# Moving operands of two FFNs laid out as even and odd tokens, and read as the two halves in turn

## The chip, the core and the metric

The kernel runs on one core of one Trainium2 chip. The metric is device time in microseconds of that core, from one launch. TensorE's records show two levels of its clock, 1.2 and 2.4 GHz; a granted clock of 1.00 in the profile is the upper one.

## What is computed

```
qn = q / (norm(q, axis=1) + 1e-6);  kn = k / (norm(k, axis=1) + 1e-6)     # 6016 x 256
a  = softmax(kn.T @ qn / tau)                                             # 256 x 256
x  = v @ a                                                                # 6016 x 256
h  = x @ w_in1;  x = (h * cos(h)) @ w_out1                                # 256 -> 2048 -> 256
h  = x @ w_in2;  out = (h * sigmoid(h)) @ w_out2                          # 256 -> 2048 -> 256
```

All inputs are float32 (the weights are handed over as 64-bit words and decoded on the chip).

## The kernel before

**Scores.** q and k stream in; 188 plain float32 matmuls (L247, moving operand 256 columns) add up the 256 x 256 score matrix. After the softmax the attention is folded into the first weights: `emit_w` (L342, plain float32, 512 columns) makes `wa` = attention times `w_in1`, so that v itself is the input of the first FFN.

**Tokens.** Everything is held transposed: features on the partitions, tokens along the free dimension. The 6016 tokens are cut into 12 blocks, four of 512 and eight of 496 tokens (`SIZES`). The moving operand of a matmul is a stretch of tokens, the stationary one a 128 x 128 tile of weights.

**Three passes.** Both FFNs compute in `float32r`, a rounded float32, with each operand split in two: `hi` is the rounded value, `lo` the rounded rest. A product is three matmuls (`PASSES`): weight hi by data hi, weight lo by data hi, weight hi by data lo. The splits of v are made on GpSimd (`split_v`; the first block's `hi` on ScalarE), those of everything later with `hi` on ScalarE (L409 in FFN 1, L441 in `part_hi`) and `lo` on VectorE (L410, L444 in `part_lo`).

**FFN 1.** A unit is (block b, m) with m = 0..7, so 96 units. `emit_h` (L381) makes two 128-row slices of h with 12 matmuls; ScalarE and VectorE form h*cos(h) and split it; `emit_o1` (L420), two units later, adds it into the output with 12 more. Each of these matmuls has a block's 512 or 496 columns. There are 4 x 8 x 24 = 768 with 512 columns and 8 x 8 x 24 = 1536 with 496.

**FFN 2.** It multiplies 2 x 2 blocks with seven products instead of eight (`PRODUCTS`), with operands formed by sums and differences (`forms_first`, `forms_second`). A block's two halves of tokens are the columns of the 2 x 2 data blocks, so a matmul (L484, in `product`) has 256 or 248 columns. `emit_x2` forms the inputs and stores them in DRAM while FFN 1 runs, `load_x2` brings them back. A unit is 7 products x 3 passes on the way in and as many on the way out: 42 matmuls, 4 x 8 x 42 = 1344 of 256 columns and 8 x 8 x 42 = 2688 of 248. The last output is finished by `emit_plain` (L523).

**Order.** The schedule is written out by hand: program order is the order in each engine's queue. Units are pipelined with a lag of two (FFN 1) or three (FFN 2), so that TensorE has the next unit's matmuls while ScalarE and VectorE work on the last one. Every matmul is preceded by the load of its own weights (PEld in the profile), which runs while the matmul ahead of it streams.

## Time and profile before

| | |
|---|---|
| median of 3 runs | 1084.74 us |
| lowest and highest | 1083.97 and 1087.33 us |
| profiled execution, first to last instruction | 1086.1 us |
| TensorE busy, share of the span | 98% |
| VectorE, ScalarE, GpSimd busy | 84%, 69%, 30% |
| mean granted TensorE clock | 0.993 |

The profiled execution's own time is given as its span alone; it lies between the lowest and the highest run. A busy share counts the time in which at least one instruction of the engine is under way. Matmuls overlap: one takes some 280 to 400 ns from its start to its end, but the next starts after 113 to 230 ns. So what a matmul costs is the time from its start to the start of the next one, which is read from the chain of waits (its pieces hold so many matmuls end to end) or from the length of a stretch divided by the matmuls in it.

### The profile page before, as it was taken

The numbers are of one execution on the slowest core, as the hardware profiler recorded it, in microseconds if no ns is written. First come the engines' busy times: TensorE is split into PE (matmuls) and PEld (weight loads), VectorE is DVE, ScalarE is ACT, GpSimd is POOL, SyncE is SP. The second block draws the span as 40 slices with busy tenths as digits, with TensorE's granted clock in tenths as the row PEclk, the third lists the DMA queues.
The fourth block names the chain that finished last, engine by engine and source line by source line (L and its number), as shares of the span: only waits on it lengthen the run. The fifth ranks groups of instructions, "written<-read, shape, count | busy, mean of one in ns | idle before, by whom it ended". The sixth has DMA issues, their size and how long they took to land.

```text
span 1086.1 us, 17011 instructions
## 1 busy us (share of the span) xinstructions
PE 1060.6 (98%) x6593; PEld 946.7 (87%) x6593; DVE 915.4 (84%) x1177; ACT 747.2 (69%) x1182; POOL 321.3 (30%) x301
## 2 busy tenths in 40 slices
PE   8888999999999999999999899999999999999998
PEld 7746788888888888888888699999999999999998
DVE  6979998878878888887677588898889889888987
ACT  6555666666666666666566578778778787787785
POOL 2257555535743455450100011111111111111110
PEclk9989999999999999999999999999999999999999
DMA  9712212243152332431127651211220220222001
GB/s 350 284 53 81 76 40 88 97 169 121 53 179 82 110 119 89 155 119 43 43 75 276 221 204 68 89 33 60 81 82 15 76 85 17 70 86 67 29 11 39
DMA packets 56544, 109.49 MB, mean 101 GB/s; under 512 B 2832, under 2 KB 37648, under 8 KB 56464
## 3 DMA queue, kind: packets, MB, share of 16 engines
q1 hardware_dynamic: 56320, 108.28, 29.3%
q8 instruction: 52, 0.85, 0.3%
q14 instruction: 28, 0.23, 0.1%
q10 hardware_dynamic: 144, 0.13, 0.0%
HBM read 68.75 MB, written 39.65 MB: 100 GB/s over the span
## 4 chain that ended last, share of the span: by engine, by line
PE 89%; DVE 8%; ACT 1%; DMA 1%; issue 0%; SPq 0%; DVEq 0%; ACTq 0%
PE h L381 23%; PE o L420 22%; PE o L484 21%; PE xz L484 12%; PE ys L484 9%; DVE acc L275 2%; PE pw L342 1%; DVE lo L410 1%; DMA qk<-qk_dram 1%; DVE t L394 1%; DVE t L402 1%; DVE wv_wo L140 1%; DVE wv_wo L144 0%; DVE wv_wo L141 0%; SPq L259 0%
## 5 line engine op out<-in xcount | busy, mean ns | idle before, releaser
L444 DVE TENSOR_TENSOR lo<-t,hi 128x744 fp32r<-128x744 f32 (+3 forms) x190 | 208.1, 1096 | 44.5 <-ACT hi L441 42.9
L484 PE MATMUL o<-hi,wo 128*128 128x248 f32 (+1 forms) x1330 | 238.6, 278 | 0.0
L381 PE MATMUL h<-xhi,wa 128*128 128x496 f32 (+1 forms) x768 | 207.9, 393 | 2.8 <-DVE wa L350 2.8
L436 POOL TENSOR_TENSOR t<-t 128x248 f32<-128x248 f32 (+1 forms) x94 | 68.3, 727 | 476.6 <-DVE t L435 421.4
L420 PE MATMUL o<-hi,wo 128*128 128x496 f32 (+1 forms) x768 | 206.6, 391 | 0.0
L441 ACT ACTIVATE hi<-t 128x744 fp32r<-128x744 f32 (+3 forms) x190 | 178.7, 941 | 40.2 <-PE o L484 39.5
L484 PEld LDWEIGHTS o<-hi,wo 128*128 128x128 f32 x1330 | 201.9, 189 | 0.0
L393 ACT ACTIVATE t<-h 128x992 int32<-128x992 f32 (+1 forms) x96 | 96.8, 1008 | 132.8 <-PE h L381 126.7
L394 DVE SCALAR_TENSOR_TENSOR t<-t,h 128x992 f32<-128x992 int32 (+1 forms) x96 | 114.9, 1197 | 84.3 <-ACT t L393 83.8
L484 PE MATMUL o<-lo,wo 128*128 128x248 f32 (+1 forms) x665 | 184.8, 278 | 0.0
L381 PEld LDWEIGHTS h<-xhi,wa 128*128 128x128 f32 x768 | 145.1, 189 | 34.9 <-ACT wv_wo L136 3.6
L420 PEld LDWEIGHTS o<-hi,wo 128*128 128x128 f32 x768 | 144.6, 189 | 30.7
L401 ACT ACTIVATE t<-t,half_pi 128x992 f32<-128x992 f32 (+1 forms) x96 | 109.1, 1137 | 65.3 <-DVE t L394 65.3
L484 PE MATMUL xz<-x2hi,wi 128*128 128x248 f32 (+1 forms) x768 | 146.6, 278 | 0.0
L410 DVE TENSOR_TENSOR lo<-t,hi 128x992 fp32r<-128x992 f32 (+1 forms) x96 | 135.3, 1409 | 1.2 <-ACT hi L409 1.2
L484 PEld LDWEIGHTS o<-lo,wo 128*128 128x128 f32 x665 | 125.5, 189 | 0.0
L420 PE MATMUL o<-lo,wo 128*128 128x496 f32 (+1 forms) x384 | 119.4, 392 | 5.6 <-DVE lo L410 5.6
L402 DVE TENSOR_TENSOR t<-h,t 128x992 f32<-128x992 f32 (+1 forms) x96 | 115.1, 1199 | 6.9 <-ACT t L401 1.2
L381 PE MATMUL h<-xlo,wa 128*128 128x496 f32 (+1 forms) x384 | 119.1, 392 | 0.0
L484 PEld LDWEIGHTS xz<-x2hi,wi 128*128 128x128 f32 x768 | 116.8, 189 | 0.2
L484 PE MATMUL ys<-x2hi,wi 128*128 128x248 f32 (+1 forms) x576 | 113.6, 279 | 3.1 <-ACT u L758 2.7
L484 PE MATMUL xz<-x2lo,wi 128*128 128x248 f32 (+1 forms) x384 | 106.8, 278 | 0.0
(129 smaller groups left out, 1660.4 us busy)
## 6 DMA issues: line engine op xcount, KB each, us to landing
qk<-qk_dram SPq DMA_DIRECT2D x22, 512.0 KB, 8.5
raw_wo<-w_out_dram SPq DMA_DIRECT2D x16, 512.0 KB, 5.2
xshi<-yhi SPq DMA_DIRECT2D x8, 868.0 KB, 6.2
xslo<-ylo SPq DMA_DIRECT2D x8, 868.0 KB, 6.6
x2hi<-xshi SPq DMA_DIRECT2D x8, 868.0 KB, 5.3
x2lo<-xslo SPq DMA_DIRECT2D x8, 868.0 KB, 7.6
wo_dram<-stage_wo SPq DMA_DIRECT2D x7, 896.0 KB, 4.7
wo<-wo_dram SPq DMA_DIRECT2D x7, 896.0 KB, 7.4
```

The costliest lines, as they stand in the source:

```text
L275: nc.vector.tensor_tensor(out=acc[:, :n], in0=acc[:, :n], in1=sq[:, :n], op=ALU.add)
L381: nc.tensor.matmul(hp[:, s, :n], lhsT, rhs, start=(i == 0), stop=(i == len(todo) - 1))
L393: nc.scalar.activation(k, hp[:, :, :n], AF.Copy, scale=1.0 / TWO_PI, bias=0.25)
L394: nc.vector.scalar_tensor_tensor(out=t[:, :, :n], in0=k, scalar=-TWO_PI, in1=hp[:, :, :n], op0=ALU.mult, op1=ALU.add)
L401: nc.scalar.activation(t[:, :, :n], t[:, :, :n], AF.Sin, bias=half_pi)
L402: nc.vector.tensor_tensor(out=t[:, :, :n], in0=hp[:, :, :n], in1=t[:, :, :n], op=ALU.mult)
L410: nc.vector.tensor_tensor(out=lo[:, :, :n], in0=t[:, :, :n], in1=hi[:, :, :n].bitcast(F32), op=ALU.subtract)
L420: nc.tensor.matmul(o[:, e, :n], wo1_at(i, f)[:, e * P : (e + 1) * P], parts[k][:, s, :n], start=(f == 0 and (i, k) == PASSES[0]), stop=(f ...
L436: eng.tensor_tensor(out=t[:, 7, :c], in0=t[:, 3, :c], in1=t[:, 6, :c], op=ALU.subtract)
L441: nc.scalar.activation(hi[:, sl, :c], t[:, 1:][:, sl, :c], AF.Copy)
L444: nc.vector.tensor_tensor(out=lo[:, sl, :c], in0=t[:, 1:][:, sl, :c], in1=hi[:, sl, :c].bitcast(F32), op=ALU.subtract)
L484: nc.tensor.matmul(out, w[:, p, ka - 1], x[r][:, kb - 1, : out.shape[-1]], start=(start and i == 0), stop=(stop and i == 2), skip_group_ch ...
```

## The change

`hi` and `lo` of every FFN matmul get another order in SBUF. Before, column j of the operand is token j of the stretch. After, the first half of the stretch holds the even tokens 0, 2, 4, ... and the second half the odd ones. The matmul's access pattern then reads element 0 of the first half, element 0 of the second, element 1 of the first, and so on, so that TensorE gets the tokens in their old order; results in PSUM, everything behind them and the output are where they were.

Three views do it. `turns` is the source in a split, read with a step of two elements (8 bytes): first the even ones, then the odd ones. `halves` is the same tile's destination, each half written contiguously. `columns` is what the matmul reads: the inner dimension has 2 elements that lie half a stretch apart (1024 or 992 bytes in FFN 1, 512 or 496 bytes in FFN 2), the outer one steps by 4 bytes.

```
+    def columns(t):
+        return t.rearrange("p (h b) -> p b h", h=2)
+    def halves(t):
+        return t.rearrange("p s (h b) -> p s h b", h=2)
+    def turns(t):
+        return t.rearrange("p s (b h) -> p s h b", h=2)
...
-            nc.scalar.activation(hi[:, :, :n], raw[:, :, :n], AF.Copy)
+            nc.scalar.activation(halves(hi[:, :, :n]), turns(raw[:, :, :n]), AF.Copy)
...
-                out=hi[:, :, :n], in0=raw[:, :, :n], scalar1=1.0, scalar2=1.0, op0=ALU.mult, op1=ALU.mult
+                out=halves(hi[:, :, :n]), in0=turns(raw[:, :, :n]), scalar1=1.0, scalar2=1.0, op0=ALU.mult, op1=ALU.mult
...
-            todo = [(wa_at(i, a, 2 * m + s), x[k][:, a, :n]) for i, k in PASSES for a in range(CH)]
+            todo = [(wa_at(i, a, 2 * m + s), columns(x[k][:, a, :n])) for i, k in PASSES for a in range(CH)]
...
-        nc.vector.tensor_tensor(out=lo[:, :, :n], in0=t[:, :, :n], in1=hi[:, :, :n].bitcast(F32), op=ALU.subtract)
+        nc.vector.tensor_tensor(
+            out=halves(lo[:, :, :n]), in0=turns(t[:, :, :n]), in1=halves(hi[:, :, :n]).bitcast(F32), op=ALU.subtract
+        )
...
-                parts[k][:, s, :n],
+                columns(parts[k][:, s, :n]),
...
-        nc.scalar.activation(hi[:, sl, :c], t[:, 1:][:, sl, :c], AF.Copy)
+        nc.scalar.activation(halves(hi[:, sl, :c]), turns(t[:, 1:][:, sl, :c]), AF.Copy)
...
-                x[r][:, kb - 1, : out.shape[-1]],
+                columns(x[r][:, kb - 1, : out.shape[-1]]),
```

The other edits (the `lo` of `split_v` and of `part_lo`, the last unit's split, `emit_plain`) are of the same kind. The numbers of instructions, their engines, their order, their sizes and the transfers stay as they were.

## Rows read from the trace of the kernel before

**Rows 1.** The page: busy time of each engine, and the granted clock in 40 slices.
```profile
PE 1060.6 (98%) x6593; PEld 946.7 (87%) x6593; DVE 915.4 (84%) x1177; ACT 747.2 (69%) x1182; POOL 321.3 (30%) x301
PEclk9989999999999999999999999999999999999999
```

**Rows 2.** The page: the chain that ended last, shares by engine and by line.
```profile
PE 89%; DVE 8%; ACT 1%; DMA 1%; issue 0%; SPq 0%; DVEq 0%; ACTq 0%
PE h L381 23%; PE o L420 22%; PE o L484 21%; PE xz L484 12%; PE ys L484 9%; DVE acc L275 2%; PE pw L342 1%; DVE lo L410 1%; DMA qk<-qk_dram 1%; DVE t L394 1%; DVE t L402 1%; DVE wv_wo L140 1%; DVE wv_wo L144 0%; DVE wv_wo L141 0%; SPq L259 
```

**Rows 3.** The chain in time order: start us, us, what, and how many.
```profile
128.72 2.75 PE h L381 x12
...
271.54 2.72 PE h L381 x12
...
595.22 2.72 PE o L420 x12
...
684.46 1.44 PE o L484 x12
...
723.63 1.44 PE o L484 x12
...
839.78 1.39 PE o L484 x12
...
992.69 1.39 PE o L484 x12
```

**Rows 4.** Busy time by stage: length, then PE, PEld, DVE, ACT, POOL, clock, DMA.
```profile
50.00:120.00 70.00, 58.90 (x209) 39.68 (x207) 63.51 (x71) 35.74 (x46) 45.29 (x39) 0.93 0.26 80
...
128.72:255.06 126.34, 126.34 (x553) 103.67 (x553) 108.58 (x104) 82.96 (x86) 64.69 (x53) 1.00 0.25 85
271.54:597.94 326.40, 326.40 (x1441) 270.03 (x1441) 260.37 (x247) 207.06 (x213) 118.15 (x94) 1.00 0.33 112
...
812.50:1073.25 260.75, 260.75 (x2294) 260.75 (x2293) 233.06 (x389) 207.30 (x444) 38.86 (x54) 1.00 0.17 51
```

**Rows 5.** Two stretches of three FFN 2 units each, 256 columns: length, PE, clock, DMA.
```profile
655.25:670.18 14.93, 14.93 (x128) 1.00 0.19 77
670.18:684.46 14.28, 14.28 (x128) 1.00 0.06 20
```

**Rows 6.** Timeline of PE: start us, us, then line, tiles, shape and count.
```profile
39.67 4.91 PE L247 MATMUL S<-qk 128*128 128x256 f32 x22
...
45.93 0.95 PE L286 MATMUL N<-ones,acc 128*128 128x1 f32 x8
46.74 2.84 PE L247 MATMUL S<-qk 128*128 128x256 f32 x12
49.41 1.95 PE L318 MATMUL pt<-ones 128*128 128x128 f32 x16
```

**Rows 7.** Groups by line and shape: busy us, mean ns of one, idle before.
```profile
L247 PE MATMUL S<-qk 128*128 128x256 f32 x188 | 43.7, 395 | 3.8 <-DMA qk<-qk_dram 3.6
...
L318 PE MATMUL pt<-ones 128*128 128x128 f32 x16 | 1.9, 275 | 0.0
```

**Rows 8.** Groups of 512 elements, ACT and DVE: L136 and L144 read 8-byte steps.
```profile
L744 ACT ACTIVATE t<-t 128x512 f32<-128x512 f32 x32 | 20.3, 633 | 0.8 <-DVE t L704 0.7
...
L136 ACT ACTIVATE wv_wo<-raw_wo 128x512 f32<-128x512 f32 x16 | 10.5, 655 | 0.0
...
L144 DVE SCALAR_TENSOR_TENSOR wv_wi<-raw_wi,wv_wi 128x512 int32<-128x512 int32 x8 | 5.5, 692 | 0.3
...
L430 DVE TENSOR_TENSOR y<-y 128x512 f32<-128x512 f32 x4 | 2.7, 682 | 0.0
```

**Rows 9.** The same view: the two VectorE splits of a unit in FFN 2.
```profile
L444 DVE TENSOR_TENSOR lo<-t,hi 128x992 fp32r<-128x992 f32 x63 | 75.1, 1192 | 28.4 <-ACT hi L441 27.1
...
L444 DVE TENSOR_TENSOR lo<-t,hi 128x744 fp32r<-128x744 f32 x63 | 61.0, 968 | 0.0
```

## The prediction, as it was put on record

> **What bounds the kernel now.** I read the page first, for which engine is never idle: PE is busy 98% of the span, and the clock is granted in full in nearly every slice [rows 1]. A busy PE is not yet the bound, since matmuls overlap, so the chain of waits comes second: 89% of it is PE, nearly all in the three FFN lines L381, L420 and L484 [rows 2]. The reader is to see there that outside the prologue nothing but the matmuls' own pace sets the end. Third, the pace itself. In the chain's time order the pieces of FFN 1 follow each other without a gap: 46 pieces of 12 matmuls between 128.72 and 255.06 us, 120 between 271.54 and 597.94 [rows 3, 4]. That is 126.34 / 552 = 228.9 ns per matmul of 512 columns and 326.40 / 1440 = 226.7 ns per one of 496. In FFN 2 a block is 336 matmuls: 684.46 to 723.63 us gives 116.6 ns for 256 columns, and four blocks from 839.78 to 992.69 us give 113.8 ns for 248 [rows 3]. With the counts of the loops: 768 x 0.2289 + 1536 x 0.2267 + 1344 x 0.1166 + 2688 x 0.1138 = 176 + 348 + 157 + 306 = 987 us of the 1086.1. Any change of these four paces goes into the time nearly whole.

> One thing more is to be seen in the paces. At 2.4 GHz, 496 columns at one per clock would be 206.7 ns; they take 544 clocks, 48 more. 512 take 549, 37 more; 248 take 273, 25 more. Plain float32 has no such loss: 22 score matmuls of 256 columns take 4.91 us, of which the last one is 0.395, so the step is 4.515 / 21 = 215 ns or 516 clocks, two per column and 4 more [rows 6, 7]. And among the 256-column matmuls of FFN 2 three units run at 14.93 / 126 = 118.5 ns and the next three at 14.28 / 126 = 113.3 [rows 5], with the same shapes, engines and clock; what differs is the index m, so which weight tile is read, and the slow ones come back after one block (a piece of 1.44 us at 684.46 and again at 723.63 [rows 3]). I read this as operand reads that just about keep up with one float32 column per clock, with stalls that depend on addresses, and keep up easily with one per two clocks.

> **The change part by part.**

> *Order and counts.* Nothing is added, removed or moved between queues; DMAs have the same sizes. Cost nothing.

> *The splits* read their source with an 8-byte step. Rows with that step exist: the decode's ACT read takes 655 ns for 512 elements against 633 for a contiguous one, the decode's DVE operation with one such operand 692 against 682 [rows 8]. So +3% and +1.5%. On the two VectorE splits of an FFN 2 unit (1.19 + 0.97 us [rows 9]) this is 0.03 us, on ScalarE's some 0.06. Per unit of 4.78 us VectorE has 0.5 us and ScalarE 1.0 us to spare (busy 233.06 and 207.30 of 260.75 [rows 4]), so the matmuls hide it; uncovered it would be 96 x 0.03 = 3 us. GpSimd's splits are 12 blocks on an engine that is busy 30% [rows 1]. I take nothing; the other end is that the extra dimension halves VectorE's rate, which is a rival below.

> *The matmuls' reads* are the change: 6336 matmuls whose neighbouring columns now lie 496 to 1024 bytes apart. No row shows a matmul that reads so; every moving operand of the kernel is contiguous. The bounds: below, the stalls may vanish, since two streams at half the speed meet the weight load differently. FFN 1 would fall to one column per clock (206.7 and 213.3 ns), 1536 x 20.0 + 768 x 15.6 = 43 us. FFN 2 has a floor under it, its weight loads: eight matmuls of a single column take from 45.93 to 46.74 us, 101 ns each, and 128 plain columns come every (1.95 - 0.275) / 15 = 111.7 ns [rows 6, 7]. With the latter as the floor FFN 2 gives back 2688 x 2.1 + 1344 x 4.9 = 12 us, 1031 us in all; at one column per clock (103.3 and 106.7 ns) it would be 42 us, and 1001 us is the lower end. Above, a fetch that used to bring several neighbours brings one column. The nearest row for a slower supply of float32 columns at the full clock is the plain float32 one, 0.840 ns per column. At that pace 512, 496, 256 and 248 columns take 430, 417, 215 and 208 ns, and the kernel gains 768 x 201 + 1536 x 190 + 1344 x 98 + 2688 x 94.5 = 154 + 292 + 132 + 254 = 832 us. Of this the first block hides some: between 50 and 120 us PE is idle 11 us, waiting for VectorE [rows 4].

> Between ends this far apart I take the upper one. A contiguous stream already misses one per clock by 7 to 10%, so there is no reserve, and the edit takes away the one thing that makes a contiguous stream cheaper to supply than a scattered one. **The sum: 1086 + 832 - 11 = 1907 us.** The profiled span is 0.1% above the median of the runs, so I leave it there.

> [...]

> **The rivals.**

> 1. *Same time: the read doesn't care where a column lies.* The 48 extra clocks would then have to come from something else than the moving stream, such as weight load or output. For it: engines with an 8-byte step lose 1 to 3%. Against it: the units at 113.3 and 118.5 ns, which differ in addresses alone. Time: 1083 to 1089 us. [...]

> 2. *Faster: the stalls go.* Place: all four paces. Two half-speed streams could hide the stall of the one behind the other, and no longer collide with the weight load. For it: the stalls follow addresses, so an order with fewer exists; three units of eight have it. Against it: scattered reads are more places per unit of time, not fewer. From half the loss to all of it, with the floor of 111.7 ns: 1059 to 1031 us; it decides as soon as an FFN 1 matmul of 496 columns comes under 225 ns.

> 3. *Slower by less: extra stalls, not a halved rate.* If the penalty falls only where the weight load reads too, some 113 of every 227 ns, then during that time half as many columns pass: 496 columns take 113 + (496 - 135) x 0.417 = 264 ns, 512 some 270, 248 some 160 and 256 some 164. That is 1536 x 37 + 768 x 41 + 2688 x 46 + 1344 x 47 = 275 us, 1361 us in all. In the same class lies VectorE at half speed in the splits: +2.2 us on a unit's 4.3 us makes 6.5 against 4.78, 96 x 1.7 = 160 us more, 1246 us; rows 8 speak against it.

> 4. *Slower by more:* a column every four clocks would double the matmuls again, some 3700 us. No row speaks for it.

> **How the numbers follow.** Halved rate 0.36, slower by less 0.16, by more 0.05, same 0.15, faster 0.28. Within 0.3% is about what a measurement of this kernel can't tell from no change. Predicted is the halved rate, 1907 us; its own range is 1880 to 1935 (11 us more or less of cover, 1% on the pace). The range over all cases leaves out the doubled case and part of the fastest: 1035 to 1935 us. It is wide because the one unknown price has ends on both sides. Slower 0.57, same 0.15, faster 0.28.

> **What would show it.** Right: matmuls of 496 columns 417 ns apart in the chain, of 248 some 208; the chain still PE; VectorE and ScalarE busy times as before, but near half the share; the 113.3 and 118.5 ns units alike. A pace of 429 and 417 in FFN 1 with FFN 2 unchanged would mean that the distance in bytes counts. Wrong: a 496-column step at 227 (rival 1), near 207 (rival 2) or near 264 (rival 3); or VectorE's L444 at 2 us with PE waiting for it.

## The result, and the profile after

The changed kernel takes 1061.55 us (median of 4 runs, 1060.61 to 1062.51) against 1085.36 us before: the ratio is 0.978, 95% interval 0.976 to 0.979. It is faster by 24 us, where 822 us slower was forecast. The profiled execution's span is 1058.8 us, against 1086.1, and the mean granted clock is 0.993 in both, so the clock has no part in the difference.

The functions are the same with other line numbers: L381 is now L392 (FFN 1 in), L420 is L433 (FFN 1 out), L484 is L500 (FFN 2), L409 and L441 (ScalarE's `hi`) are L420 and L454, L410 and L444 (VectorE's `lo`) are L421 and L457.

The page of the changed kernel, busy times and the chain that ended last:

```profile
PE 1020.2 (96%) x6593; PEld 939.2 (89%) x6593; DVE 940.4 (89%) x1177; ACT 807.6 (76%) x1182; POOL 331.2 (31%) x301
...
PE 66%; DVE 19%; ACT 9%; issue 4%; DMA 1%; SPq 0%; DVEq 0%; ACTq 0%
```

TensorE's busy time fell by 40 us, ScalarE's rose by 60 and VectorE's by 25, and the chain, which was 89% PE [rows 2], is 66% PE. Two things happened, and the chain in order of time shows both (start us, us, what, how many):

```profile
176.43 2.59 PE h L392 x12
...
254.59 3.28 PE h L392 x12
...
270.58 2.51 PE h L392 x12
...
646.82 1.31 ACT hi L454
...
651.85 1.31 ACT hi L454
...
656.89 1.29 ACT hi L454
...
840.13 1.34 PE o L500 x12
...
844.82 1.34 PE o L500 x12
```

Twelve matmuls of 512 columns take 2.59 us where they took 2.75, so 216 ns each instead of 229; twelve of 496 take 2.51 instead of 2.72, 209 instead of 226.7 [rows 3]. An FFN 2 unit of 248 columns takes 844.82 - 840.13 = 4.69 us, 111.7 ns per matmul instead of 113.8. So every pace of TensorE is better. But the FFN 1 blocks of 512 got almost nothing from it: the first 496-column matmuls start at 254.59 us, before at 255.06 [rows 4], since TensorE waits in between, most of all for VectorE's `lo` (L421). And in FFN 2's 256-column blocks a unit takes 651.85 - 646.82 = 5.03 us, more than the 39.17 / 8 = 4.90 of before [rows 3], with the chain on ScalarE and VectorE by turns. The groups by shape name the reason (busy us, mean ns of one, idle before); first the changed kernel's, then those of the kernel before:

```profile
L420 ACT ACTIVATE hi<-t 128x992 fp32r<-128x992 f32 x64 | 74.0, 1156 | 2.6 <-DVE t L413 1.9
...
L420 ACT ACTIVATE hi<-t 128x1024 fp32r<-128x1024 f32 x32 | 50.7, 1584 | 0.8 <-DVE t L413 0.2
L454 ACT ACTIVATE hi<-t 128x1024 fp32r<-128x1024 f32 x32 | 44.3, 1385 | 0.0
...
L457 DVE TENSOR_TENSOR lo<-t,hi 128x1024 fp32r<-128x1024 f32 x32 | 41.4, 1295 | 16.3 <-ACT hi L454 15.8
...
L433 PE MATMUL o<-lo,wo 128*128 128x512 f32 x128 | 41.0, 403 | 13.6 <-DVE lo L421 13.5
```

```profile
L409 ACT ACTIVATE hi<-t 128x992 fp32r<-128x992 f32 x64 | 65.7, 1026 | 1.3 <-DVE t L402 1.3
...
L409 ACT ACTIVATE hi<-t 128x1024 fp32r<-128x1024 f32 x32 | 33.7, 1055 | 0.2
...
L441 ACT ACTIVATE hi<-t 128x1024 fp32r<-128x1024 f32 x32 | 33.9, 1059 | 0.0
...
L444 DVE TENSOR_TENSOR lo<-t,hi 128x1024 fp32r<-128x1024 f32 x32 | 39.2, 1225 | 16.2 <-ACT hi L441 15.8
...
L420 PE MATMUL o<-lo,wo 128*128 128x512 f32 x128 | 40.5, 398 | 5.6 <-DVE lo L410 5.6
```

For 992 elements `hi` takes 1.16 us, for 1024, only 3% more, it takes 1.58 and 1.39; before it took 1.03, 1.06 and 1.06. VectorE's `lo` of 1024 elements grew too, if less: 1295 ns against 1225 in FFN 2, and in FFN 1 a mean of 1742 against 1559. TensorE's wait for `lo` in FFN 1 grew from 5.6 to 13.6 us.

### The profile page after: what moved, and what is told of

The parts are those of the page before. It is cut to its first block, busy times and chain, and to the rows that moved or that the text cites. A ratio compares the mean times of both kernels' runs of the same rounds, so it can differ in the third digit from the quotient of the medians.

```text
span 1058.8 us, 17011 instructions
## 1 busy us (share of the span) xinstructions
PE 1020.2 (96%) x6593; PEld 939.2 (89%) x6593; DVE 940.4 (89%) x1177; ACT 807.6 (76%) x1182; POOL 331.2 (31%) x301
## 4 chain that ended last, share of the span: by engine, by line
PE 66%; DVE 19%; ACT 9%; issue 4%; DMA 1%; SPq 0%; DVEq 0%; ACTq 0%
PE o L433 18%; PE h L392 18%; PE o L500 14%; PE xz L500 8%; PE ys L500 6%; ACT hi L454 4%; DVE lo L421 3%; DVE acc L286 2%; ACT t L760 2%; DVE t L443 2%; DVE t L405 2%; DVE t L413 2%; DVE lo L457 1%; DVE t L719 1%; PE pw L353 1%
## 5 line engine op out<-in xcount | busy, mean ns | idle before, releaser
L457 DVE TENSOR_TENSOR lo<-t,hi 128x744 fp32r<-128x744 f32 (+3 forms) x190 | 212.8, 1121 | 39.0 <-ACT hi L454 37.8
L500 PE MATMUL o<-hi,wo 128*128 128x248 f32 (+1 forms) x1330 | 232.6, 275 | 0.0
L454 ACT ACTIVATE hi<-t 128x744 fp32r<-128x744 f32 (+3 forms) x190 | 208.0, 1095 | 16.9 <-PE o L500 16.0
L500 PEld LDWEIGHTS o<-hi,wo 128*128 128x128 f32 x1330 | 202.2, 192 | 0.0
L392 PE MATMUL h<-xhi,wa 128*128 128x496 f32 (+1 forms) x768 | 195.1, 377 | 3.0 <-DVE wa L361 3.0
L433 PE MATMUL o<-hi,wo 128*128 128x496 f32 (+1 forms) x768 | 196.0, 378 | 0.1
L500 PE MATMUL o<-lo,wo 128*128 128x248 f32 (+1 forms) x665 | 183.2, 275 | 0.0
L392 PEld LDWEIGHTS h<-xhi,wa 128*128 128x128 f32 x768 | 146.1, 190 | 21.6 <-issue 4.3
L433 PEld LDWEIGHTS o<-hi,wo 128*128 128x128 f32 x768 | 146.6, 191 | 17.8 <-POOL wv_wo L147 0.5
L421 DVE TENSOR_TENSOR lo<-t,hi 128x992 fp32r<-128x992 f32 (+1 forms) x96 | 147.6, 1537 | 5.9 <-ACT hi L420 5.8
L500 PE MATMUL xz<-x2hi,wi 128*128 128x248 f32 (+1 forms) x768 | 144.2, 276 | 0.0
L433 PE MATMUL o<-lo,wo 128*128 128x496 f32 (+1 forms) x384 | 116.2, 385 | 13.8 <-DVE lo L421 13.8
L500 PEld LDWEIGHTS o<-lo,wo 128*128 128x128 f32 x665 | 127.8, 192 | 0.0
L420 ACT ACTIVATE hi<-t 128x992 fp32r<-128x992 f32 (+1 forms) x96 | 124.7, 1299 | 3.5 <-DVE t L413 2.2
L500 PE MATMUL ys<-x2hi,wi 128*128 128x248 f32 (+1 forms) x576 | 115.1, 282 | 7.1 <-ACT u L774 4.5
L500 PEld LDWEIGHTS xz<-x2hi,wi 128*128 128x128 f32 x768 | 117.1, 193 | 0.1
L392 PE MATMUL h<-xlo,wa 128*128 128x496 f32 (+1 forms) x384 | 112.5, 375 | 0.0
```

The lines of the kernel that those rows point to most:

```text
L392: nc.tensor.matmul(hp[:, s, :n], lhsT, rhs, start=(i == 0), stop=(i == len(todo) - 1))
L420: nc.scalar.activation(halves(hi[:, :, :n]), turns(t[:, :, :n]), AF.Copy)
L421: nc.vector.tensor_tensor(out=halves(lo[:, :, :n]), in0=turns(t[:, :, :n]), in1=halves(hi[:, :, :n]).bitcast(F32), op=ALU.subtract)
L433: nc.tensor.matmul(o[:, e, :n], wo1_at(i, f)[:, e * P : (e + 1) * P], columns(parts[k][:, s, :n]), start=(f == 0 and (i, k) == PASSES[0]), ...
L454: nc.scalar.activation(halves(hi[:, sl, :c]), turns(t[:, 1:][:, sl, :c]), AF.Copy)
L457: nc.vector.tensor_tensor(out=halves(lo[:, sl, :c]), in0=turns(t[:, 1:][:, sl, :c]), in1=halves(hi[:, sl, :c]).bitcast(F32), op=ALU.subtract,)
```

## The experiments

**E1: the read alone.** Contiguous splits as before, only the matmuls read in turn:

```
     def halves(t):
-        return t.rearrange("p s (h b) -> p s h b", h=2)
+        return t
     def turns(t):
-        return t.rearrange("p s (b h) -> p s h b", h=2)
+        return t
```

> Operands are laid out as before the change (contiguous tokens, contiguous splits); only the matmuls read the two halves in turn, so the tokens of the output come in another order. Theory A (neighbouring float32 columns read one per clock stall; taking them from places far apart ends it, and the new splits cost time on ScalarE): steps as in the changed kernel, 209 ns for 496 columns, 216 for 512, 112 in FFN 2, and ScalarE's hi back at 1.03 us (992 elements) and 1.06 us (1024); time 1086 - 37 - 12 = some 1037 us, under the changed kernel. Theory C (the gain comes from the layout or the splits, not from the read): steps of 227 and 229 ns, 1085 us.

Measured: 1043.27 us, ratio 0.961 (0.959 to 0.962). A chain piece of FFN 1 and the two groups of ScalarE:

```profile
401.41 2.51 PE h L392 x12
...
L420 ACT ACTIVATE hi<-t 128x992 fp32r<-128x992 f32 x64 | 65.6, 1024 | 2.4 <-DVE t L413 2.0
L420 ACT ACTIVATE hi<-t 128x1024 fp32r<-128x1024 f32 x32 | 33.8, 1055 | 1.2 <-DVE t L413 0.7
```

The read alone gains 42 us; with the new splits beside it 18 of these are lost. Theory C is out. The sum of the paces had promised 49 us; the PE that is faster waits 7 us more for others (span less busy time 32.6 us, before 25.5).

**E2: the split alone.** The layout of the changed kernel, read straight through:

```
     def columns(t):
-        return t.rearrange("p (h b) -> p b h", h=2)
+        return t
```

> Operands are laid out as even and odd tokens, but the matmuls read them straight through, so the tokens of the output come in another order. Theory A: steps of 227 (496), 229 (512) and 113 to 119 ns (FFN 2) as before the change; ScalarE's hi takes 1.15 us and more instead of 1.03; time 1085 us or some us over it. Theory C: 209 and 216 ns, some 1060 us. If the slower hi (1.16 to 1.58 us) comes from the matmuls reading in turn at the same time, hi is back at 1.03 us here; if it comes from its own 8-byte step, it stays slow.

Measured: 1085.0 us, ratio 0.9996 (0.9986 to 1.0005).

```profile
L420 ACT ACTIVATE hi<-t 128x992 fp32r<-128x992 f32 x64 | 70.8, 1107 | 1.3 <-DVE t L413 1.3
...
L420 ACT ACTIVATE hi<-t 128x1024 fp32r<-128x1024 f32 x32 | 36.4, 1139 | 0.1
```

The 8-byte step by itself costs ScalarE 8% (1107 against 1026, 1139 against 1055), and the matmuls, slow as before, hide it. The 1584 ns of the changed kernel come neither with this alone nor with E1's read alone (1055), but with both together.

**E3, E6, E8: other orders of reading.** One kernel each, contiguous operands; every block of tokens has its own order, so one profile holds many. The kernels as a whole, one run each, take 1265.92, 1185.99 and 1237.05 us. The matmuls' operand goes through this (in E3 without the two lines for `thin`):

```
    def columns(t, b):
        kind = KINDS[b]
        if kind == "row":
            return t
        if kind[0] == "turns":
            return t.rearrange("p (h b) -> p b h", h=kind[1])
        if kind[0] == "step":
            return t.rearrange("p (b h) -> p h b", h=kind[1])
        if kind[0] == "thin":
            return t.rearrange("p (h b t) -> p t b h", h=2, t=kind[1])
...
        if kind[0] == "near":
            return t.rearrange("p (b h t) -> p b t h", h=2, t=kind[1])
        return t.rearrange("p (h b t) -> p b h t", h=2, t=kind[1])
```

> Operands contiguous as before the change; each block's matmuls read them in another order, so the tokens of the output come in another order. 512 columns: block 1 straight, block 2 halves in turn, block 3 two neighbouring runs of 4 in turn (0,4,1,5,...). 496 columns: block 4 straight, 5 halves in turn, 6 evens then odds (step 8 bytes), 7 step 16 bytes, 8 order 0,2,1,3, 9 order 0,4,1,5, 10 pairs from the two halves in turn, 11 runs of four from the two halves in turn. FFN 1 step for 496 columns. Theory A (neighbours in time must not be neighbours in memory): 209 ns in blocks 5 to 9, 227 in block 4, and between in 10 and 11. Theory B (two half-speed streams far apart dodge the weight load): 209 only in blocks 5, 10 and 11; steps of one stream (6, 7) and near orders (8, 9) stay at 227.

Measured, pieces of the chain of E3, blocks 4 to 11 in their order:

```profile
276.15 2.72 PE h L405 x12
292.47 2.51 PE h L405 x12
...
360.09 5.28 PE h L405 x12
...
455.74 5.36 PE h L405 x12
...
514.77 2.72 PE h L405 x12
...
562.88 2.51 PE h L405 x12
...
616.36 3.89 PE h L405 x12
...
661.05 2.83 PE h L405 x12
```

Both theories fall. A and B had 209 ns, the one or the other, in blocks 6, 7, 8, 10 and 11, and none of these has it. The read in two neighbouring runs of four (block 9) is as good as the one in far halves, the evens and then the odds (block 6) is nearly twice as slow as straight, and 0,2,1,3 (block 8) is exactly as slow as straight. What orders these results is not the distance of neighbours but, it seems, **every second column**: take the columns at even places of the order as one stream, those at odd places as another. Suppose lines of four columns (16 bytes), which E8 was to test. Straight (227 ns), a stream goes 0, 2, 4, 6 and makes two accesses to a line; in turn (209 ns) it goes 0, 1, 2, 3 and makes four; with evens first (440 ns) it goes 0, 4, 8 and makes one. This is theory D, which E6 and E8 had to foretell numbers with.

> As e3, contiguous operands read in other orders. Theory D (the columns at even and at odd places of the order are two streams; a stream is at full pace when four accesses in a row fall into one 16-byte line, loses some 8% with two, and runs at half pace with one) against theory A (only neighbours in time must not be neighbours in memory). FFN 1 step for 496 columns: block 4, runs of eight in turn (0,8,1,9,...): D 209, A 209. Block 5, quarters in turn (0,q,2q,3q,1,...): D 317 to 440, since a stream changes its line at every access; A 209. Block 6, evens of the two halves in turn, then the odds: D 227, A 209. Block 7, every fourth of the two halves in turn: D 440, A 209. Block 8, runs of eight straight from the two halves: D some 230. Block 9, halves in turn again: 209; blocks 10 and 11 straight: 227. 512 columns: block 2 as 4: 216; block 3 as 5: D over 320, A 216.

Measured, E6's blocks 4 to 9 and 10:

```profile
281.12 2.51 PE h L409 x12
...
331.48 3.16 PE h L409 x12
...
367.31 2.64 PE h L409 x12
...
430.66 5.28 PE h L409 x12
...
489.10 2.81 PE h L409 x12
...
549.30 2.51 PE h L409 x12
...
580.25 2.72 PE h L409 x12
```

Block 7 decides: the two halves in turn, but each only at every fourth token, run at 440 ns; the places are as far apart as in the changed kernel, and theory A wanted 209. Blocks 4, 8 and 9 came as D had them; blocks 9 and 10 repeat orders of E3 (209 and 227 ns), so a block's place in the kernel doesn't matter. Block 5 (quarters) is slower than 209 as D wanted, but 263 and not over 317, and block 3, the same with 512 columns, 278 and not over 320; block 6 is 220 where D had 227. So a change of line at every access costs, but less when the stream goes between two lines and comes back (263 ns for quarters, against 440 where it doesn't come back); D has the order, not these sizes.

> Contiguous operands, read in two runs of four in turn (0,4,1,5,...) as in e7 without the permuting split, so the tokens of the output come in another order; in FFN 1 the operands of some blocks start 1 to 4 elements later in their tiles. Theory D with lines of 16 bytes that lie at fixed addresses: FFN 1 step for 496 columns 209 ns in blocks 4 (no offset) and 8 (offset 4), some 225 in block 6 (offset 2, every run is cut two and two), and between 209 and 330 in blocks 5 and 7 (offsets 1 and 3, cut one and three). Block 9 (straight, offset 2) 227, block 10 (halves in turn, offset 2) 209 to 212. Block 2 (512, eighths in turn) and block 11 (496, eighths in turn): over 263, since a stream goes through four lines in turn. Theory A' (no lines; only the distance between neighbours counts): 209 in blocks 4 to 8 and 10 and 11 alike.

The edit gives FFN 1's operands a start inside their tile:

```
+OFF = [0, 0, 0, 0, 0, 1, 2, 3, 4, 2, 2, 0]
...
-        hi = flat(sc.tile([P, NU, HB], F32R, tag="hi", name=f"hi1_{b}_{m}"))
+        hi = flat(sc.tile([P, NU, HB], F32R, tag="hi", name=f"hi1_{b}_{m}"))[:, :, OFF[b] :]
```

Measured, E8's blocks 4 (no offset), 5 (one), 6 (two), 7 (three), 8 (four) and 11 (eighths):

```profile
311.77 2.51 PE h L410 x12
...
365.62 3.12 PE h L410 x12
...
396.39 2.69 PE h L410 x12
...
452.43 3.12 PE h L410 x12
...
497.40 2.51 PE o L451 x12
...
667.79 5.37 PE h L410 x12
```

| order (h, q: a half, a quarter of the columns away) | stream at even places | a line's accesses, in a row or in turn | ns |
|---|---|---|---|
| halves in turn; 0,4,1,5,...; 0,8,1,9,... | 0,1,2,3 | 4 in a row | 209 |
| evens of both halves in turn, then odds | 0,2,4,6 | 2 in a row | 220 |
| 0,4,1,5,... started two elements later | 0,1 / 2,3 | 2 in a row | 224 |
| straight; 0,2,1,3 | 0,2,4,6; 0,1,4,5 | 2 in a row | 227 |
| runs of eight, of four, from both halves | 0,2,4,6 / h,...; 0,2 / h,h+2 | 2 in a row | 234, 236 |
| 0,4,1,5,... started one or three later | 0 / 1,2,3 | 1 and 3 | 260 |
| quarters in turn | 0,2q,1,2q+1 | 4, two lines in turn | 263 |
| pairs from both halves | 0,h,2,h+2 | 2, two lines in turn | 324 |
| every fourth of both halves; evens, then odds | 0,4,8 | 1 | 440 |
| step of 16 bytes; eighths in turn | 0,8; four lines in turn | 1; 4 | 447, 448 |

**E4: reading and writing in pairs.** An attempt to have the gain without the splits, with the output in PSUM written in the same order as it is read; the splits are contiguous as in E1:

```
     def columns(t):
-        return t.rearrange("p (h b) -> p b h", h=2)
+        return t.rearrange("p (h b t) -> p b h t", h=2, t=2)
...
-                nc.tensor.matmul(hp[:, s, :n], lhsT, rhs, start=(i == 0), stop=(i == len(todo) - 1))
+                nc.tensor.matmul(columns(hp[:, s, :n]), lhsT, rhs, start=(i == 0), stop=(i == len(todo) - 1))
...
-                o[:, e, :n],
+                columns(o[:, e, :n]),
```

FFN 2's outputs are edited the same way.

> Operands contiguous, splits as before the change; matmuls read pairs of tokens from the two halves in turn and write their PSUM output in the same pairs, so that everything keeps its place and the output its order. If pairs are enough and PSUM takes pairs at full pace: steps of 209, 216 and 112 ns, some 1037 us. If pairs count as neighbours (theory A strictly): 227 ns and 1085 us. If PSUM writes in pieces cost time: steps over 229 ns and a time above 1090 us.

Measured: 1500.13 us, ratio 1.381 (1.375 to 1.386).

```profile
508.52 3.81 PE h L392 x12
```

318 ns per 496 columns, what E3's block 10 has for reading pairs alone (324). So it is the read that is dear. The expectation had put a time above 1090 us down to the writes; that the output goes to PSUM in pairs doesn't show beside so slow a read, and what it would cost beside a fast one is not shown.

**E5: blocks of other sizes.** The changed kernel with one line edited:

```
-SIZES = 4 * [512] + 8 * [496]
+SIZES = 4 * [504] + 8 * [500]
```

> The changed kernel with blocks of 504 (four) and 500 tokens (eight) instead of 512 and 496, so that no two halves lie 1024 or 512 bytes apart. Theory F (ScalarE's slow hi in the changed kernel, 1.38 to 1.58 us for 1024 elements against 1.16 for 992, comes from halves at a power-of-two distance that TensorE reads in turn while ScalarE reads with its 8-byte step): hi takes some 1.17 us in all blocks, TensorE waits no more in the first four blocks, and the time is some 1045 us. Theory G (it comes from the length of the tile or from where it starts): hi stays over 1.35 us in the longer blocks and the time at 1060 us.

Measured: 1040.75 us, ratio 0.959 (0.958 to 0.960), 21 us under the changed kernel.

```profile
L454 ACT ACTIVATE hi<-t 128x1008 fp32r<-128x1008 f32 x32 | 37.1, 1160 | 0.0
```

`hi` of 1008 elements takes 1.16 us in FFN 2; of 1024 it took 1.39 in the changed kernel. So ScalarE's slow `hi` hangs on the halves being 1024 or 512 bytes apart (theory F). VectorE's `lo` goes with it: 1208 ns for FFN 2's 1008 elements, where the changed kernel had 1295 for 1024. What the reads gave in the first four blocks was taken back by these two together; no run parts them.

**E9: the split into halves, but a near read.** The changed kernel with `columns` as in E7 below.

> The changed kernel with its split into halves, but the matmuls read two neighbouring runs of four in turn, so the tokens of the output come in another order. Steps 209, 216 and 112 ns. If ScalarE's slow hi of 1024 elements (1.58 and 1.39 us) needs TensorE at two places 1024 or 512 bytes apart (theory F), it is 1.14 to 1.16 us here as in e2, and the time some 1043 us; if any full-pace read beside an 8-byte step does it, it is 1.4 us or more and the time some 1060 us.

Measured: 1040.25 us in its one run.

```profile
L457 DVE TENSOR_TENSOR lo<-t,hi 128x1024 fp32r<-128x1024 f32 x32 | 39.2, 1224 | 11.9 <-ACT hi L454 11.9
...
L454 ACT ACTIVATE hi<-t 128x1024 fp32r<-128x1024 f32 x32 | 36.4, 1139 | 0.0
```

With the same sizes and the same splits, but TensorE reading two places 16 bytes apart, `hi` is back at E2's 1.14 us and `lo` at 1224 ns. So the slow `hi` needs all three: ScalarE's own 8-byte step (E1 has none), TensorE reading two places in turn (E2 doesn't), and 1024 or 512 bytes between these (1008 and 504 don't do it, nor do 16).

**E7: two neighbouring runs of four in turn.** The order of E3's block 9 everywhere; the four layers of matmuls then leave one permutation inside groups of eight, which the split of v takes back:

```
     def columns(t):
-        return t.rearrange("p (h b) -> p b h", h=2)
+        return t.rearrange("p (b h t) -> p b t h", h=2, t=4)
...
+        for a in range(CH):
+            h, l = [t[:, a, :n].rearrange("p (g h t) -> p g h t", h=2, t=4) for t in (hi, lo)]
+            r = raw[:, a, :n].rearrange("p (g t h) -> p g h t", h=2, t=4)
```

> All matmuls of both FFNs read two neighbouring runs of four in turn (0,4,1,5,2,6,3,7) from contiguous operands. Each of the four layers so permutes the tokens inside groups of eight; the permutation has order three, so four layers leave one of it, which the split of v on GpSimd (and ScalarE for the first block) takes back by writing evens and odds of eight. No other split changes, and the output has its order. Theory D: steps of 209, 216 and 112 ns, ScalarE's hi at 1.03 and 1.06 us, GpSimd's split of v dearer but hidden; some 1043 us as in e1, 18 us under the changed kernel. If the run of four in GpSimd's writes makes its split late, TensorE waits at the start of a block and the time is above 1050 us.

Measured: 1039.18 us, ratio 0.958 (0.957 to 0.959). The page and two groups:

```profile
PE 1009.4 (97%) x6593; PEld 935.0 (90%) x6593; DVE 919.5 (89%) x1177; ACT 748.0 (72%) x1183; POOL 326.4 (31%) x324
...
L453 ACT ACTIVATE hi<-t 128x1024 fp32r<-128x1024 f32 x32 | 33.8, 1055 | 0.0
...
L216 POOL TENSOR_SCALAR xhi<-vraw 128x496 fp32r<-128x496 f32 x16 | 17.3, 1079 | 70.5 <-DMA vraw<-vT_dram 64.4 <-PE h L391 6.1
```

This is the lowest time of the study, 22 us under the changed kernel, though E5 and E9 are within 2 us of it. ScalarE's busy time is as before the change. GpSimd's split of v became two instructions per tensor and stays hidden.

## Why the prediction was wrong

**What bounds the kernel** was read rightly: the matmuls' paces set the end, and the paces moved it. That the losses of 48 and 37 clocks come from operand reads, which follow addresses, was right for 42 and 31 of them: in the changed kernel 496 and 512 columns take 209.2 and 215.8 ns (2.51 and 2.59 us by 12). In FFN 2, where units stood at 113.3 and 118.5 ns, all go at some 111.7 once nothing holds them up (248 columns in the changed kernel; in E1 the 144.00 us from 602 to 746 us hold 1292 matmuls, most of them of 256 columns, 111.5 ns each).

**The step that failed** is the choice between the ends: "the edit takes away the one thing that makes a contiguous stream cheaper to supply than a scattered one". It took for granted that two columns that follow each other in time share a fetch. E3, E6 and E8 fit a supply in which a column shares it with the next but one. Straight reading gives two accesses to a line (227 ns for 496 columns), the changed order four (209 ns); the change that looked like scatter was the better neighbourhood. The price itself, one column per two clocks, exists: 440 ns, against 417 in the forecast, in the orders with one access to a line. It was put on the wrong order. That the measured 1061.55 us lie within the range of 1035 to 1935 is no merit of the forecast: the range spans both ends, and faster had a chance of 0.28.

Counted column by column, the changed order has a new line at each column, and by that count the matmuls had to pay. The runs show lines of 16 bytes (E8) and 440 ns with one access to a line, but the accesses count within every second column, and two of them are not yet full pace for float32r: 220 to 236 ns with two, 209 with four.

**Rival 2** is what happened, with two streams at half speed as it had them, but hardly for its reason: two neighbouring runs (E3's block 9, 209 ns) do as well as two far halves, and whether the weight load had any part is not shown. Its prices held for the read: 43 us for FFN 1 less the 2.5 ns by which each matmul stays above its columns' time (209.2 ns over 206.7, 215.8 over 213.3) makes 37, and FFN 2 stopped at the 111.7 ns that the 128-column matmuls had given as a floor. Its range, 1059 to 1031 us, holds E1's 1043.27; the whole change lies above it because of the splits.

**Rival 1** had the read not care where a column lies. It does: by their order and start alone, 496 columns take 209 to 448 ns. In the changed kernel twelve matmuls of 512 columns take 2.59 us and twelve of 496 take 2.51, which is 0.417 ns for each further column; 209.2 ns is 496 of these and 2.5 ns. So in FFN 1 a matmul is its columns and a small constant after the change, with four accesses to a line, and not before (226.7 ns). For FFN 2's 248 columns the same sum gives an estimate of 105.8 ns, where 111.7 is measured.

**The splits** were mis-sized. Forecast was +3% on ScalarE from the decode's 655 against 633 ns, hidden. Alone it is +8% (E2), still hidden; with the matmuls in turn it is +13% at 992 elements and +50% and +31% at 1024, and then ScalarE and VectorE, no longer the matmuls alone, set the pace in four of twelve blocks. That took 18 us of the 42. VectorE's share held in the other eight blocks, where its `lo` of 992 and 744 elements in FFN 2 takes 1193 and 968 ns as before [rows 9]; in the first four it is +6% at 1024 (1295 against 1225), not +1.5%. The prediction took the splits and the reads as independent; what they cost together was in no row of before.

**Slower by less and by more** found no place in this kernel. Orders of the first kind exist (260 to 324 ns); of the second, a column every four clocks, none was found: the slowest take 448 ns for 496 columns. Rival 3's 113 of every 227 ns, in which the weight load reads, were the author's estimate: one load lasts 189 ns in the records of before (L381), and no run parts its reads from the moving operand's.

Open are three things: why straight reading costs 42 clocks at 496 columns and 31 at 512 when both have two accesses to a line, why it depended on the weight tile in FFN 2 (113.3 and 118.5 ns), and what ScalarE and VectorE share with TensorE that a distance of 512 or 1024 bytes makes them slower. E5 and E9 show that it does, not how. The supply in two streams orders all the paces measured, but it was made up after E3, and of E6's sizes it missed three.

## What to carry to other kernels

Where TensorE's pace is the bound, compare the step between matmuls with columns by clock (here 226.7 ns with 206.7); a loss that depends on addresses may be ordered away, as here (209.2 ns), and a kernel in which each block reads in another order prices a dozen orders in one profile. Look for the order that is free to produce: a permutation inside groups of eight, which the split of v undoes, cost no time that shows (E7, 1039.18 us, the lowest), while the halves, read far apart, cost ScalarE 60 us of busy time. And when a gain on the bounding engine is larger than what arrives, look at the next engine by shape: ScalarE's `hi` of FFN 2 has a mean of 1095 ns over all shapes (L454), which hid a group at 1385.

## What the runs showed that was not expected

- float32r columns are supplied as if by two streams, the even and the odd places of the order, each in lines of 16 bytes: 209 ns per 496 columns with four accesses to a line in a row, 220 to 236 with two, 440 to 447 with one.
- Moving an operand by one element (4 bytes) takes a matmul from 209 to 260 ns, by two to 224, by four back to 209.
- ScalarE's copy with an 8-byte step takes 1.14 us for 1024 elements (E2), but 1.39 and 1.58 in the changed kernel, while TensorE reads in turn at places 512 and 1024 bytes apart; for 1008 elements with 504 and 1008 bytes between the places (E5) it is 1.16 us. VectorE's `lo` of 1024 elements goes from 1225 to 1295 ns in the same place, and is back at 1224 when TensorE reads 16 bytes apart (E9).
